# Paired softmax reciprocals, a common PSUM ring, QKV buffers for the first transform steps and a new task order

## The chip, the cores and the metric

The kernel runs on one core of one Trainium2 chip. Times are device microseconds of one execution. Runs come with a label: slow, when a run is over 1.5% above the fastest of the same kernel. On this kernel the times of one program spread evenly over some 2 to 3%, so that label cuts through one cloud; I give medians of all runs, and the ratios of fast runs beside them.

## The reference

Two independent halves share the output. Half A is a long convolution: a kernel K of 2048 taps for each of 1024 channels is built from complex exponentials, and u is convolved with it. Half B is attention in which each position sees 8 earlier ones at distance 2.

```python
P = jnp.exp(logdA[:, :, None] * l[None, None, :])
K = jnp.einsum("dn,dnl,dn->dl", Cc, P, dB).real
y = irfft(rfft(pad(K)) * rfft(pad(u)))[:L] + u * Dskip           # half A
q, k, v = split_heads(x @ wqkv)                                   # half B, 32 heads of 32
attn = softmax(where(mask, (q * k_gathered).sum(-1) * scale, -1e9))
out = concat([y, (attn @ v_gathered) @ wo], axis=-1)
```

## The kernel before

One program does both halves at once, as tasks put on the engines in a fixed order that is stored as a string (`ORDER`). The first part does the QKV projection (writing q, k, v to memory) beside the generation of K. A "shift" matmul group then finishes K, and a transform is done as matmuls: step 1 for u and for K (the tiles `z`), spectral products with constants `m` (`fwd`, product, `back`), and a last step. The attention (scores, exp, mask, values, reciprocal, product, output projection) is mixed into the spectral work.

```python
# first transform step, one group: 4 matmuls into a two-bank PSUM tile, then a copy
w["pz"] = cp().tile([128, 4, 256], F32, name="cp")
for i in range(4):
    nc.tensor.matmul(w["pz"][:, i, :], lhsT=src["t"][:, :, 4 * pi + i], rhs=self.l1[:, lk], ...)

# softmax denominators of one channel tile: exp(-ln(sum)), with a check sum
nc.scalar.activation(out=ln[:], in_=u["O"][:, 1, :], func=ACT.Ln, bias=self.tiny[:])
nc.scalar.activation(out=ln[:], in_=ln[:], func=ACT.Exp, scale=-1.0, accum_out=self.sums[:, 1, i:i + 1])
nc.vector.tensor_tensor(out=st["oT"][:, ct, :], in0=u["O"][:, 0, :], in1=ln[:], op=ALU.mult)

# constants of a spectral group: three buffers, loaded by GpSimd's queue
w["m2"] = self.mid.tile([128, 768], BF, name="m2", bufs=3)
nc.gpsimd.dma_start(out=w["m2"][:], in_=self.m2[p])
# [cut]
```

PSUM, eight banks: while QKV runs, three two-bank tiles (`ps`) for it and one (`cpl`) for the transform; afterwards two (`cp`) and one (`cpl`) in common and two single banks for attention's values.

Of the kernel before, what the change touches and what calls it, by code (L numbers as in the profile page):

```python
# [28 lines left out]
class Plan:  # L29
# [31 lines left out]
    "CQARAFwAgQE5AIkBIQAAAFAAlAGZAUEAGABpAWQAKQAdAmwASAAlAnEBMADsAPkBAQJID3wBoQFNAlEB0ADkABEC+AAMAlUCdQLwAAABDAEtAqEPqA8wAskB4QFgAn0CdAAYDrEBqAFZAbEPuA9AAngAiABkAYAA"  # L61
    "lADRATgCmADpAVEPWA/cAfQBSA7IDtwAEAFhD2gPcA+kAJ0CwA8cAagAuQEgAeEQoQ6lArQAxAEsAcAAvADoEPEQOAGoDlgCsQ4hDswA+Q4oDvgQNAF5DgAPgAIAEUQBMQ64DoAOqAKwAogCSAEZEMAOTAMJDzgO"
    "QA64AokOEA8YD5AOyQ8gENAPaAKQAsACyQLVAuAC3QLoAv0CJQMIAzAD8AIFA10DEAMtA0ADKRAwEHkPOAMYA4UDZQOQA2gDcAO1A5gOjQNVA1EOvQM4EMAD2Q/gD5gDgA/IA60DWA6JD6ADIQ+QD5gP/APoDywE"
    "2QM5EWEO5AMoD2gOcA4JBOwDMQ80BAQE0ANBBDgPOAR4A0AR0Q5ADyUF8Q/4D9gOSRFQES0FHARVBTUFCBHwA8kFSQThDlgRuRDoDvAOQRAUBDgFXARdBQEQCBDAEEgFQAVgBX0FaAVUBIgFyRCREBAQcAWlBUgQ"
    "hQVYEq0F1QVMBlEQuAWYBZEEkAWwBeAFaQSYBHAEeARhEcAF/QWABN0FWBDwBSUGoASYECAECAboBQUGXQYYBi0GEAZoBqgEiRGFBjgGuATQEGUGsATYEIgEcAYwBo0GQAZoEWAQwQSQEVUGcRHpBCAWyARgBPAE"
    "eAbQBPgEtQa9BtgE/AaQBqEQeBGAEQAFEAWoEMAGmAbIBpkRrQagEagRBAcREdkG4ATYERgFLAfQBuwGNAcJBzgH5AYlCGkQGBGwEPAGcBB5EIAQoAZhEmgSFAchEdkSQQfhEYgQLQjgEhwHcRKxEegRSQcoEQgF"
    "MBFcBzgIVQhUB8kI6RJpB3gSgBJdCJEHfQhgCDUICRJICEwJcAeYB2gIpQiICPEReAdACKAHhQhwCNUI4B6YCLAI8BKQCPgRrQjACLgI4AgBE4AHqAf9CN0IsAeIB+gICBMlCfgSBQnBBzAJEAm4EbgH8AhVCV0J"
    "LQnpBwASyAcQEggJwRHIEdAR8AcYCTgJ0AcxEvgHQAllCXAJGRJgB4UJkAloCY0JtQkgEtgHmAkgBwAICAgQCL0JERP8CcgJKBIYE60JIBM4EtETwAnQCUESSBJQEhgIKBYECikT2BPZCckL4RPoEzATCQosCjQK"
    "ORNAE4kSoAkhFDgKeAnsCSUL5AmgExwKkBLwEy0LQQoUCvAJmRJREygUWBN5E0kKoBJIE1UL4Ac4CzULSAtAC1wKVAqoEmALYRM1FGAKkQp9C2gTXQtpCrESpQtwC2gLhQuwC3AKiAs4FJgKoAqQC9ULmAutC8AL"
    "OBa4C3gKuBKACuAL/QvdC+gLJQyYFHATBQwIDIgKgBONExgM8AtAFMESyBKoCrAKqRNMDBAMMAyQE5gTXQxxFC0MOAy4CukKhQyNDEAM0BKYDMEKaAyQDLAT8Aq1DGUM6B6hFCAKyAqoFL0MyAygDNAKMBbADHAM"  # L70
    "uRPZDFUMeBR4DAkNgRT8DPgK0AzAE9gK+RMEDeQM7AzwDBwN8BUZFkAWQQ3IExQNABRMDVQNiBRJFJAUAAsQC+AKsRRQFBgLCAu4FGENiQ2tDGgNCRSQDcAUyRSYDXANoA14DSwNgA00DagN0BRAFeENuQ3oDcAN"
    "EBRxFRgUyA3wDdAN+A1ZFBAO8B7YDQAOWA2wDQgOOA0gDegVUhZZFjEXCBZaF0wWYRaFFogWkBb9FgAXSRXZFGAXGhggGHgVDB8IF6oXYBRoFIEVUBXgFLQXyheIFc0W6BTQFhkVWRXUF/oXIBUAGOoXkBUpFTAV"
    "8RT0FwoYtRbYFhAYYBWZFTgVaBW6F8AX+BTaFxUXwRXgFzoXuBagFQEVQBcYF4oX+B4IFRAVkBfIFWoX5RboFqkVcBfAFnoXnRagFtEVsBUgF4AXbRZwFpoXoBfwFkoXUBdAGLgV2BXgFSoYOBj4FWwqqRiwGDQY"
    "ABZpGBoZdBggGTkZiRiQGOoYRBlJGFAY9BjZGNoe+hgAGXkY5BiEGKkZqBYpGTAZChkUGbkYwBiZGKQYWRpaGGAYyRhYKnEqeSqBKkgZ1BiqKlEZsRlZLLEqwRnIGYwquRnKK2EacRrRK7wqkSrUGZkreBbdGWoa"
    "eBpZGaErhBqZKsEqjRppGeEZcBnpGQEaySpiGXwZkRqlKpkaCSvcK/AZEh+FGRErrCshHwka4SsZH9Qq6SvZKuEqCRscK4oZsSv4GbkrGRokGhEa9CshK6AalRlgKtUfxCuoGigaNRpFH+wqaStxKxIbIRsoG7Ea"
    "GRswGz0bfCuYGTkrQStMKzoa8SpBGvkqBCspKzQroBlhG4EtQRu6Go0fiS1IGsEayRpRK9Aa2BpqG7kbTRt5G1AbWBvlGnEbgSthLIAb6hpQGlkrjBtpLPEs8RpkK5Ub+SxIH8Eb0RsQFmkcyhv4GgAb+CvgG5kb"
    "2B8RHNwbcRx0LO0boRt6HPEb4B+ULYEciSuMHJAcUB+ZLZQrkSwaHPkbKRyQH50cmSwwHKgbLR95LCEcPBxFHMEcgSyhHMoc2RyNLLAbpCwZHSksMB/gHKEt0hypHL0fMCwAHDksCBxJHFEcwB+sLZgfIR0xHewc"
    "9RywHDgdcR2yLfkcBC1ALLktuBwFHQktKR0RLUgsRB1YHMkdCB0iLSktxC15HaksgR0cLVItAB+JHZAdmB3IH00dyS3RHaUdUR1ZLWAc4R3oHTgfsSylH7ws2h3wHV0fASyqHdEtdR8ILFkdeR4QHbUdZC1pLcEs"
    "gh4RLJEeIR79HckseB/ULJgeKR45HjEeSB6KHtAeRB6oHxgsYB+kHvEfaSBwIBkgACE6ICQgUCxAIIkhGSEgIZQh6iCpIDQt8CCZIdwtoCG0IHEtCiE5LSkgMCAUIbkh2iDgIEEuxCFJLnwtUS7pIfAhrR5aIWQh"
    "mS+4HaEvYB3ZLNkhICy5IEEtwCB6IOQhaSGEIMAdSSBwIWovSSFxL5ogVCCsL4kgaB1QIUwt4C0BHqAg4SxcLpQgyiApMA0esR5VHtAguR5ZIAogEB4YHikhYCAwIWEuFCA5IWkuRCF6LskhqSF1LoEu7CzQIREi"  # L80
    "tCH6HwAgsS95IfkhfC8IIvgguS+EIVoeACLZLuEujC5pImUegS8ZInEixC8pIjAigSKMIkoowB4iIpEuOCLsLnkiCS/IHpkulCJQKBIuWCgRL4kvpC6ZJ2gfOS/BIkEvySIcL6gnoCdoHnAeRSLZIuAiGC6dIiEu"
    "SSJRIugfcSOUL1giYCLRIkwvIS/yMPEuqS4pL+wiYCihIiguMC40L7EuvC5RL3kjiSMZI/kw+S5oKK0i6i2BI5AjMTAELzkw9SLwLVkvnCPBLiEjOC75IvktAC4xI7AiBDG4IkQwISQ4Iyoj0ShkL6UjSTCwJ8ku"
    "BSMII0AjcSgQI9Qu3ShRMHko4CgJMU0jCC5iMGkwdDCpI5EwsSO4I8Aj6CjSL5kwITERMV0wUSMpMVkjeTApJDkkgTA0McgvpDDJI9EkHDHYL+EvRCQxJIAoTCTZJKkwgjGxKIww6STwJBEyuCeJMbAf0SO5KOgv"
    "4iT4JDkxVSThI2Aj2SPsI7EwwTD0I/ovlDHJMPAvQTG8MFEx1DBMMVkkmTF5JFkx/SPAKGEkoTEFJdkwGTJkMWgjITI5M0EzADABJKwx4TAJJAkzDTBoJEwzLDLsMGkxKSURM4IkkSQQJCAwnCRwJAklcTGIKIkk"
    "ESUQMDEyMiUcMxgkOTJBJaQkfDFFMiEoOSVIJS0oUTOBJXoyUCWBMiEzSTIYJYklUTKtJJIlsSSZJaglpCWwMVwy2TLIKIwyWTPhMvkzvSTZJSAlujEpMzAoOCgYMGQzXSU0M2kzkTKZMsAkcTPAMckxtSWkMmEl"
    "0DFhMuwyqTJpMuEmbSWxMuIl2DF8M/EycCX5MsEn8SX8JekluiUAJs0ndDLIJAE06SaBMwk0xSXIJfEmMSZ4JfkmACfiJwgnvDIEM9AnDSbpJzE00CXBMjk0FDQRJokz8Cf4Jx0myTKUM+IxwTSAH0Q01DIZNFE1"
    "FSfoMck0WTUhNIkmkSahJhknSTRkNagmYTQgJjknIScoJggyaTT1MfgxUTQtNNQ0mia0JiE12TShM+E0dDRcNOw08jRpNfk0eTRxNb0mKTU6JtgngTSoMwEomDNJJgkoBDVUJnw1ADLhNbUzuDOMNJIokTSZNEEm"
    "KCcwJ1gmQCgJNUEnETXwKDQ1qSmdKKQ0USdcJ8ImHDXJJqk06TXxNak2ZSawKTk1EChKJ2kmsTZkJ7E0vDQ5N0E3/DVxJm0ngDVBNcozATYZNiE20DPwM7w2CTbZNsAz2TNMNcE2yTZMN+E2LDZSN7I1FTbsNlk3"
    "yTf6KBApeTbQJtQ2gTZkNzE24DOMNngm6DO4KfE2CTdJNrg1OTbYJoAmETccN3En+TZENsE1UTYAKaAokTYEN9I3fSchN8g12TfxOIAniTXAKZk2qCj5OFw2wjjkN6Q2YTYpNwQ5NDfJOJA10DXUOOo3GCkIKdg1"
    "aTZ0NvE3kjidNQk5/TcROdk4mThhOBw5cTekOKk4IjlpOOE4GCigNag1sTjIKew4vDh4N3Q4gSkpOTQ5gTeIN40pAjh5ODk5kCkxOAk4FDiBODk4mCmMONEpQTlCKU0pGThMOUQ42SmZNyIpUClYKSE4SThQOVE4"  # L90
    "XDjgKegpKSksODAptDmgNzEqOCmQN6k3sDfANz0qgjlhKbg3QCqIOUgqaSlZOfEpcCl4KZE5+SmYOQAqEioZKiAqKCpgOYgnKBegOQgqujmQJ2g3qDlpOXA5eDnEOVAqoCk="
# [403 lines left out]
RU = 256  # L495
NB = 4
# [6 lines left out]
SO = CP, ("O",) + CP  # L503
# [144 lines left out]
class Attention:  # L648
# [9 lines left out]
    def open_pools(self, ctx):  # L658
        pool = lambda n, b, **kw: ctx.enter_context(self.tc.tile_pool(name=n, side="right", bufs=b, **kw))
        cst = pool("t_c", 1); self.ld = pool("t_ld", 2); self.wk = pool("t_wk", 2); self.otp = pool("t_oT", 2)  # L660
        self.pp = pool("t_ps", 2, space=PSUM)
        self.mk = cst.tile([128, 2 * W0 + 64], BF, name="mk"); self.wo = cst.tile([128, 8, 1024], BF, name="wosb")
        self.sums = cst.tile([128, 2, 64], F32, name="sums")

    def load(self, ru, st):
        nc = self.tc.nc; f = 1 if ru % 4 == 0 else 0
        qs = self.ld.tile([128, 8, RU], BF, name="qs"); ks = self.ld.tile([128, 8, RU + 32], BF, name="ks"); vs = self.ld.tile([128, NB + 1, 512], BF, name="vs")
        nc.sync.dma_start(out=qs[:], in_=self.QT[ru])
        nc.sync.dma_start(out=ks[:, :, 32 * f:], in_=self.KT_[ru][:, :, 32 * f:])
        for h in range(2):  # L670
            nc.sync.dma_start(out=vs[64 * h:64 * h + 64, 1:, :], in_=self.Vd[ru * RU:ru * RU + RU, h, :].rearrange("(b k) x -> k b x", k=64))
            if not f:
                nc.sync.dma_start(out=vs[64 * h:64 * h + 32, 0, :], in_=self.Vd[ru * RU - 32:ru * RU, h, :])
        st.update(qs=qs, ks=ks, vs=vs)
# [14 lines left out]
    def exp(self, u):  # L689
        u["pe"] = self.wk.tile([128, 2, W0], BF, name="pe", bufs=3)  # L690
        self.tc.nc.scalar.activation(out=u["pe"][:], in_=u["S"][:, :, 0:W0], func=ACT.Exp, scale=SCALE, accum_out=self.sums[:, 0, u["i"]:u["i"] + 1])  # L691
# [5 lines left out]
    def values(self, ru, ct, st, u, bank):  # L697
        nc = self.tc.nc; first = ru % 4 == 0; ones = self.mk[:, 2 * W0:2 * W0 + 64]; pm = u["pe"]
        O = u["O"] = bank(self.pp, "O").rearrange("p (two q) -> p two q", two=2)
# [15 lines left out]
    def recip(self, u):  # L715
        ln = u["ln"] = self.wk.tile([128, RU], F32, name="ln")
        self.tc.nc.scalar.activation(out=ln[:], in_=u["O"][:, 1, :], func=ACT.Ln, bias=self.tiny[:])  # L717
        self.tc.nc.scalar.activation(out=ln[:], in_=ln[:], func=ACT.Exp, scale=-1.0, accum_out=self.sums[:, 1, u["i"]:u["i"] + 1])  # L718

    def norm(self, ct, st, u):  # L720
# [481 lines left out]
```

## Time and profile before

| | before |
|---|---|
| time | 523.11 us median of 4 runs (518.59 to 523.39) |
| span of the profiled run, clock | 517.9 us, 0.95 |
| TensorE busy | 449.4 us (87%) |
| ScalarE, VectorE busy | 406.2 us (78%), 385.2 us (74%) |
| K shift, first spectral matmul | 221.2 us, 272.4 us |

Busy shares alone would say that TensorE sets everything. The table of stages in the prediction says more: in one stretch of 51 us TensorE is slow in clock (0.83), and VectorE and ScalarE are idle for 61% and 44% of it.

### The profile page before, as it was taken

To read this page: it belongs to the slowest core of one execution; us is meant where nothing else is said; L and a number is where in the kernel's file an instruction comes from. 1 tells how busy PE (TensorE), PEld (TensorE's weight loads), DVE (VectorE), ACT (ScalarE), POOL (GpSimd) and SP (SyncE) were. 2 spreads that over 40 slices of the span, in tenths; PEclk is the share of its full clock that TensorE was granted. 3 is DMA by queue.
4 is the path that set the end of the run, shared out by engine and by line. 5 is a ranking of instruction groups with operands and counts; after the bars stand their busy time and mean duration, and the time that the engine had idled before them with its cause. 6 is when DMAs were issued, how large, how long until landed. Compare 5 with 4: busy or idle time off the path is not lost.

```text
span 517.9 us, 16566 instructions
## 1 busy us (share of the span) xinstructions
PE 449.4 (87%) x7056; PEld 238.9 (46%) x7118; DVE 385.2 (74%) x682; ACT 406.2 (78%) x738; POOL 34.8 (7%) x56
## 2 busy tenths in 40 slices
PE   4769999789999799779698788889997998998994
PEld 4544444444544345445474333476443443444541
DVE  2899999979899989515089897699773896784540
ACT  4779999996999988244769987799875986787863
POOL 1740000000000000010001010001000100000000
PEclk9979999899999899879879999999998998998998
DMA  8841333633416388545785787875779494788743
GB/s 290 274 131 45 81 88 106 140 73 118 104 48 154 93 160 251 119 131 132 173 212 127 246 207 241 272 218 145 197 223 237 128 260 131 183 235 223 223 143 108
DMA packets 110209, 86.39 MB, mean 167 GB/s; under 512 B 44896, under 2 KB 98912, under 8 KB 108848
## 3 DMA queue, kind: packets, MB, share of 16 engines
q1 hardware_dynamic: 106016, 73.91, 53.1%
q0 software_dynamic: 3024, 9.25, 6.3%
q10 hardware_dynamic: 1088, 2.10, 1.2%
q8 instruction: 57, 0.93, 0.8%
q14 instruction: 24, 0.20, 0.1%
HBM read 51.28 MB, written 33.95 MB: 165 GB/s over the span
## 4 chain that ended last, share of the span: by engine, by line
PE 34%; issue 9%; DMA 5%; DVE 5%; ACT 3%; POOL 1%; POOLq 0%; ACTq 0%
PE cp L755 8%; DMA m<-c_m 5%; PE cp L893 4%; PE ps L587 4%; PE cp L942 3%; PE cp L925 3%; PE cp L984 3%; PE O L712 3%; DVE z L467 2%; PE cp L686 2%; PE O L704 2%; ACT z L465 1%; POOL m L915 1%; DVE f L467 1%; ACT vs L465 1%
## 5 line engine op out<-in xcount | busy, mean ns | idle before, releaser
L587 PE MATMUL ps<-xT,w 128*128 128x512 bf16 x490 | 121.9, 397 | 4.9 <-ACT sg L465 2.3
L587 PEld LDWEIGHTS <-w 128*128 128x128 bf16 x512 | 50.4, 101 | 61.2 <-issue 10.7
L755 PE MATMUL cp<-wosb,oT 128*128 128x512 bf16 x232 | 59.0, 386 | 2.3 <-issue 1.4
L617 PE MATMUL ps<-wv,xT 128*128 128x512 bf16 x246 | 58.0, 381 | 2.1 <-DVE xT L467 1.2
L465 ACT CAST sg<-ps 128x1024 bf16<-128x1024 f32 x46 | 46.0, 1005 | 11.2 <-issue 5.1
L465 ACT CAST z<-cp 128x1024 bf16<-128x1024 f32 x38 | 38.0, 1014 | 18.3 <-PE cp L893 17.9
L925 PE MATMUL cp<-z,m 64*64 64x512 bf16 x512 | 39.0, 393 | 14.4 <-DMA m<-c_m 11.8
L467 DVE CAST z<-cp 128x1024 bf16<-128x1024 f32 x26 | 31.5, 1223 | 26.4 <-PE cp L893 26.1
L467 DVE CAST f<-cp 128x1024 bf16<-128x1024 f32 x28 | 34.2, 1223 | 17.7 <-PE cp L925 17.5
L893 PE MATMUL cp<-l,big 128*128 128x256 bf16 x256 | 39.8, 298 | 8.6 <-ACT z L465 5.0
L691 ACT ACTIVATE pe<-cp 128x576 bf16<-128x576 f32 x64 | 41.4, 648 | 6.3 <-PE cp L686 5.6
L465 ACT CAST f<-cp 128x1024 bf16<-128x1024 f32 x36 | 36.0, 1009 | 12.2 <-PE cp L925 11.8
L915 POOL DMA_DIRECT2D m<-c_m x32 | 17.3, 540 | 395.8 <-ACT kraw L465 188.9
L934 DVE TENSOR_TENSOR pr<-f 128x1024 bf16<-128x1024 bf16 x64 | 41.0, 684 | 1.1 <-ACT f L465 0.7
L893 PEld LDWEIGHTS <-big 128*128 128x128 bf16 x256 | 33.9, 173 | 15.6 <-issue 11.4
L617 PEld LDWEIGHTS <-xT 128*128 128x128 bf16 x256 | 24.6, 99 | 30.0 <-DVE xT L467 1.3
L695 DVE TENSOR_TENSOR pe<-pe,mk 128x576 bf16<-128x576 bf16 x64 | 28.4, 452 | 11.6 <-ACT pe L691 11.4
L755 PEld LDWEIGHTS <-oT 128*128 128x128 bf16 x256 | 23.0, 99 | 28.8 <-issue 4.8
L717 ACT ACTIVATE ln<-O,tiny 128x256 f32<-128x256 f32 x62 | 29.6, 477 | 8.1 <-PE O L712 7.9
L942 PE MATMUL cp<-pr,m 64*128 64x512 bf16 x256 | 33.7, 383 | 0.7 <-ACT f L465 0.5
L723 DVE TENSOR_TENSOR oT<-O,ln 128x256 bf16<-128x256 f32 x62 | 25.8, 419 | 10.6 <-ACT ln L718 9.6
L276 DVE SCALAR_TENSOR_TENSOR PH<-p_xs,p_phs 128x256 int32<-128x256 f32 x84 | 30.1, 419 | 0.6 <-ACT TL L285 0.6
(114 smaller groups left out, 731.1 us busy)
## 6 DMA issues: line engine op xcount, KB each, us to landing
Zv<-vs SPq DMA_DIRECT2D x64, 128.0 KB, 3.7
big<-Zv SPq DMA_DIRECT2D x32, 256.0 KB, 4.7
m<-c_m POOLq DMA_DIRECT2D x32, 192.0 KB, 3.6
Vt<-sg SPq DMA_DIRECT2D x32, 128.0 KB, 2.3
KT<-sg SPq DMA_DIRECT2D x16, 256.0 KB, 2.9
QT<-sg SPq DMA_DIRECT2D x16, 256.0 KB, 2.5
ud<-in_A_u_dram SPq DMA_DIRECT2D x16, 256.0 KB, 5.6
big<-ud SPq DMA_DIRECT2D x2, 2048.0 KB, 9.2
```

The source lines that it names most:

```text
L276: V.scalar_tensor_tensor(out=PH[:, j, :], in0=xc, scalar=float(RS[k + j] + 128), in1=self.phs[h][:, cs], op0=ALU.mult, op1=ALU.add)
L465: nc.scalar.copy(out=out, in_=in_)
L467: nc.vector.tensor_copy(out=out, in_=in_)
L587: nc.tensor.matmul(st["ps"][:, h, :], lhsT=self.w[ct // 2, t][:, kt, ct % 2 * 128:ct % 2 * 128 + 128], rhs=self.xT[:, kt, t0:t0 + 512], st ...
L617: nc.tensor.matmul(st["ps"][:, b, :], lhsT=self.xT[:, kt, t0:t0 + 128], rhs=self.wv[:, kt, :], start=(kt == 0), stop=(kt == 7))
L691: self.tc.nc.scalar.activation(out=u["pe"][:], in_=u["S"][:, :, 0:W0], func=ACT.Exp, scale=SCALE, accum_out=self.sums[:, 0, u["i"]:u["i"] ...
L717: self.tc.nc.scalar.activation(out=ln[:], in_=u["O"][:, 1, :], func=ACT.Ln, bias=self.tiny[:])
L755: nc.tensor.matmul(w["po"][:, h, :], lhsT=st["oT"][:, ct, tt * 128:(tt + 1) * 128], rhs=self.wo[:, ct, h * 512:(h + 1) * 512], start=(ct = ...
L893: nc.tensor.matmul(w["pz"][:, i, :], lhsT=src["t"][:, :, 4 * pi + i], rhs=self.l1[:, lk], start=True, stop=True, skip_group_check=True)
L925: nc.tensor.matmul(f[64 * ab:64 * ab + 64, c2, :], lhsT=t[rs, ab, o:o + 64], rhs=z[rs, 4 * p + 2 * ab + zi, :], start=(zi == 0), stop=(zi ...
L934: V.tensor_tensor(out=w["pr"][:, x], in0=w["f"][:, :, :, 0:256], in1=w["f"][:, x:x + 1, :, 256:512].to_broadcast([128, 2, 2, 256]), op=ALU ...
L942: nc.tensor.matmul(v[:, ab, :], lhsT=t[rs, k, :], rhs=w["pr"][rs, x, y].rearrange("p c d -> p (c d)"), start=(i == 0), stop=(i == 3), tile ...
```

## The change

It has four parts. (1) The denominators of two channel tiles are inverted by one Ln and one Exp, and normalised by one product; both outputs share one two-bank tile of the common ring, which gets a third `cp` buffer in place of the two single banks. (2) The first u steps may use the PSUM buffers of QKV. (3) Keys and queries are loaded in one task, V in a later one. (4) The order string is new; in it seven half-tiles of QKV (eight matmuls each) stand before the shift instead of after it.

```diff
-        self.pp = pool("t_ps", 2, space=PSUM)
-        ln = u["ln"] = self.wk.tile([128, RU], F32, name="ln")
-        activation(out=ln[:], in_=u["O"][:, 1, :], func=ACT.Ln, bias=self.tiny[:])
-        activation(out=ln[:], in_=ln[:], func=ACT.Exp, scale=-1.0, accum_out=self.sums[:, 1, i:i + 1])
+        ln = w["ln"] = self.wk.tile([128, 2, RU], F32, name="ln", bufs=LN_BUFS)      # LN_BUFS = 1
+        activation(out=ln[:], in_=w["O"][:, :, 1, :], func=ACT.Ln, bias=self.tiny[:])
+        activation(out=ln[:], in_=ln[:], func=ACT.Exp, scale=-1.0, accum_out=self.sums[:, 64 + i:65 + i])
-        tensor_tensor(out=st["oT"][:, ct, :], in0=u["O"][:, 0, :], in1=u["ln"][:], op=ALU.mult)
+        tensor_tensor(out=st["oT"][:, ct:ct + 2, :], in0=w["O"][:, :, 0, :], in1=w["ln"][:], op=ALU.mult)
 # first step
-                    w["pz"] = cp().tile([128, 4, 256], F32, name="cp")
+                    pool, n = psum(); w["pz"] = pool.tile([128, 4, 256], F32, name=n)
-                m = P("PE", 0.48, mm, [zh, l1], take=CP, ...)
+                m = P("PE", 0.48, mm, [zh, l1], take=("cpl", "ps") if hf == 0 and lk == 0 else CP, ...)
 # loads
+    def load_v(self, ru, st):      # the V part of load(), issued as its own task
-            st["cp"] = ...tile_pool(name="cp", side="right", bufs=2, space=PSUM)
+            st["cp"] = ...tile_pool(name="cp", side="right", bufs=3, space=PSUM)
 # [cut: the task list that goes with it, and the ORDER string]
```

## The prediction

> **What bounds the kernel now.** I began with the busy row and then cut the span into stages at events that the timeline shows: the start (to 39 us), QKV projection beside the generation of the convolution kernel K (39 to 208 and 208 to 221, where the last K values are drained), the first transform step with leftover QKV matmuls between (221 to 272.4, where the first spectral matmul starts), then spectral work, attention and output projection mixed until 507, and the tail. This is the stage table of the kernel before; columns are stretch, length, busy us of PE, PEld, DVE, ACT, POOL with instruction counts, granted clock, DMA share, GB/s.
>
> ```profile
> 0.00:39.00 39.00, 23.71 (x193) 18.26 (x196) 27.82 (x42) 25.11 (x33) 17.55 (x24) 0.91 0.71 231
> 39.00:208.00 169.00, 158.55 (x2284) 78.25 (x2307) 158.59 (x304) 158.21 (x258) 0.00 (x0) 0.97 0.46 113
> 208.00:221.00 13.00, 9.59 (x404) 5.71 (x405) 6.48 (x11) 2.98 (x6) 0.00 (x0) 0.87 0.50 102
> 221.00:272.40 51.40, 42.71 (x271) 28.62 (x274) 19.90 (x39) 28.60 (x32) 1.63 (x3) 0.83 0.67 165
> 272.40:340.00 67.60, 56.55 (x1048) 27.60 (x1049) 56.48 (x105) 57.16 (x107) 7.01 (x13) 1.00 0.75 219
> 340.00:403.00 63.00, 56.32 (x982) 31.38 (x976) 46.76 (x66) 50.89 (x101) 4.31 (x8) 0.97 0.75 205
> 403.00:507.00 104.00, 98.07 (x1895) 47.48 (x1916) 68.98 (x118) 80.29 (x204) 4.31 (x8) 0.97 0.68 188
> 507.00:518.00 11.00, 3.85 (x19) 1.61 (x18) 0.14 (x1) 2.94 (x3) 0.00 (x0) 0.81 0.30 103
> ```
>
> TensorE is busy 449.4 of 517.9 us, so only its 68.8 us of idle time and its slow clock can be won: 15.3 us idle in the start, 10.5 to 208, 3.4 to 221, 8.7 to 272.4, 11.1 to 340, 6.7 to 403, 5.9 to 507, 7.2 in the tail. From 39 to 208 all three engines are at 94%: nothing is free there. The stretch 221 to 272.4 is the odd one: VectorE works 19.9 of 51.4 us, ScalarE 28.6, and TensorE's clock is only 0.83. The waits of all engines and the timeline say why:
>
> ```profile
> ACT z L465 <- PE cp L893: 17.9, 20, 3.3
> DVE z L467 <- PE cp L893: 26.1, 9, 13.9
> ```
>
> The two evacuating engines sit 44 us waiting for first-step matmuls, 41.7 of them in this stretch. In the chain of waits, between 225 and 252 us, a group of four such matmuls (0.44 us) alternates with eight QKV matmuls (1.73 us): at that point the first step has one two-bank PSUM buffer, because the others open only once QKV has closed its own. From 272 on, TensorE's waits are short and mostly for the constants m:
>
> ```profile
> PE cp L925 <- DMA m<-c_m: 11.8, 12, 3.0
> ```
>
> **What the Trainium skill says.** "ScalarE: Activation LUTs", section "What ACT_TABLE_LOAD costs", gives an ACTIVATE as a fixed part plus 0.833 ns an element: a merged instruction keeps one fixed part. The trace agrees in slope: the copy of 1024 takes 1005 to 1014 ns and the Ln of 256 takes 477, 0.69 ns an element apart over different functions; I use 0.83. "VectorE: DVE Perf Modes", section "Why PSUM operands drop a tier", says fp32 from PSUM runs at the single rate; the 1024-element copy at 1223 ns and the 256-element product at 419 differ by 1.05 ns an element, which agrees. "PSUM — Partial Sum Buffer", "Specifications (TRN2)", gives eight 2 KiB banks; before, 2x2 (cp) + 2 (cpl) + 2x1 (O) use them all, after, 3x2 + 2 do. "TensorE: Matmul & The Clock Gate", "What's actually happening", says the clock is halved after an idle window; the trace shows 28 first-step matmuls taking 5.94 us (212 ns each) at 259 us, against 0.44 us for four (110 ns) earlier.
>
> **The change, part by part.** These are the rows concerned, from the groups by shape:
>
> ```profile
> L717 ACT ACTIVATE ln<-O,tiny 128x256 f32<-128x256 f32 x62 | 29.6, 477 | 8.1 <-PE O L712 7.9
> L718 ACT ACTIVATE ln<-ln 128x256 f32<-128x256 f32 x64 | 26.7, 417 | 2.0
> L718 ACT ACTIVATION_READ_ACCUMULATOR ln<-ln 128x1 f32 x64 | 11.9, 186 | 0.0
> L723 DVE TENSOR_TENSOR oT<-O,ln 128x256 bf16<-128x256 f32 x62 | 25.8, 419 | 10.6 <-ACT ln L718 9.6
> ```
>
> *Pairs.* One tile costs ScalarE 477 + 417 + 186 = 1080 ns, 64 tiles 69.1 us. A pair should cost (477 + 256x0.83 = 690) + (417 + 213 = 630) + 186 = 1506 ns, 32 pairs 48.2 us: 20.9 us less ScalarE work, about 5 us in 272 to 340, 16 us after. The VectorE product goes from 64x419 = 26.8 to 32x(419 + 256x1.05 = 688) = 22.0 us, 4.8 us less. TensorE's instructions are the same in number and shape. As TensorE is the bound, this is no 21 us of span; it buys shorter waits in the 23.7 us of idle time between 272.4 and 507. PSUM: the one-bank outputs go, two tiles share a two-bank buffer of a common ring with one buffer more. A pair holds it from its first value matmul through about 1.5 us of reciprocal and 0.7 us of product, some 4 us with the second tile's matmuls; 32x4 = 128 us over four buffers in 235 us leaves the rest the equivalent of 3.5 buffers instead of 3. This is a mild gain, with the danger that a held pair blocks the ring.
>
> *First u steps.* They may also take the QKV buffers (three more), and the order moves QKV ahead. Counted in TensorE's program order: after the K shift, 11 half-tiles of eight QKV matmuls stand between first-step groups before, 4 after; 7 half-tiles, 7x1.73 = 12.1 us, move to before 221 us. The stretch after the shift then holds 4x1.73 + 128x0.11 + about 2 for the shift = 23 us of TensorE work at full clock instead of 35. Evacuation for it (32 z tiles, about 18 on ScalarE and 14 on VectorE, 4 of QKV, the K placements of about 6 us on VectorE) is 22 us of ScalarE and 23 of VectorE. With start and fill latencies I take 32 us instead of 51.4: 19.4 won. The 12.1 us must be paid before 221, where TensorE idled 13.9 us since 39. Much of that idle time is the wait for K's producers or too early to fill; I let 4 us go into it, so the shift comes 8 us later. Net 11 us.
>
> *Keys and queries apart from V.* Scores can start on a load of two tensors while V follows. No large wait of TensorE on these loads is listed before, so I give it nothing by itself; it makes the other order possible.
>
> *New order in the spectral part.* The load of m has three buffers, so group p+3's load starts when group p's inverse matmuls are done. I added up TensorE work lying between these points, using the matmul spacings of the trace (0.07 us forward, 0.12 inverse, 0.216 projection): before, 15 of 29 loads have under 5 us of cover, after, 14, the missing sum falls from 23.0 to 18.5 us, and the last 16 have 7.7 us of cover on average instead of 6.5. Landing takes 2.6 to 8.3 us, so I take 2 us of the 11.8 away. From slack on ScalarE, the fourth buffer and a little more clock I take another 4 us. Net 6 us here.
>
> Sum: 11 + 6 = 17 from about 521 us (the runs before lie at 518.6 to 523.4), so 504. The new order is dense and I know none of its waits; I give back 2 us for waits that I can't name and predict 506.
>
> **Rivals.** (1) *The work moved ahead isn't absorbed.* From 39 to 208 TensorE, ScalarE and VectorE are all at 94%, and the QKV drains move with the matmuls (about 3.5 us of ScalarE). If none of the 12 us fits, and the last K values come later still through ScalarE, the first part gains 5 us or less: 511 to 514. For it: the 94%. Against it: the 13.9 us idle, and that 208 to 221 was slow through clock 0.87, not through ScalarE at 3 of 13 us. (2) *The pair becomes the wait.* Two tiles must be ready for one Ln, the ln tile now has one buffer, and a held two-bank output stalls scores and forward matmuls behind it. If each of 32 pairs costs TensorE 0.4 us, 13 us go: 517 to 519, about the time of before. For it: in the new order the two value groups of a pair are up to 3.2 us of TensorE work apart. Against: most lie within 0.4 to 1.6 us, and successive pairs start 5 us apart on average. (3) *DMA holds the second half.* The DMA share is 0.68 to 0.75 there and the bytes don't change; if waits for m and for the round trip of Zv through memory stay as they are, all of the 6 us fail: 510 to 512. (4) *All idle time but the start and tail shrinks by half*, as smoother feeding also lifts the clock from 0.83: 498.
>
> **Range and chances.** 2% under 521 is about 511. The central path and rival 4 lie below it, rival 3 on it, rivals 1 and 2 above. None of them gets above 523 unless two meet. I take 497 to 516 as the range for 8 in 10, 0.66 for faster, 0.31 for the same, 0.03 for slower.
>
> **What would show it.** Right: Ln near 690 ns and the second Exp near 630, 32 of each; the stretch from the K shift to the first spectral matmul at 30 to 35 us with the waits of ScalarE and VectorE on first-step matmuls well under 25 us together; the shift at 225 to 231 us; TensorE's idle time between first spectral matmul and 11 us before the end at 16 to 19 us, TensorE's total busy time within 1% or lower. Wrong: the shift later than 233 us (rival 1); TensorE waiting over 8 us on the Ln, the normalising product or a buffer they hold (rival 2); waits for m at 12 us or more (rival 3).

## The result

The changed kernel takes 507.06 us (median of 4 runs, 502.91 to 512.25) against 523.11. The ratio of the fast runs is 0.9686 (95% interval 0.9597 to 0.9775). A ratio here is the mean time of one kernel's fast runs over that of the other's in the same rounds, so it isn't quite the ratio of the medians.

The stage table of the changed kernel has the same columns as that of before. Its shift comes at 224.7 us and its first spectral matmul at 252.9 us, so the cuts lie there; the next two stretches are as long as before.

```profile
0.00:39.00 39.00, 21.53 (x184) 16.47 (x185) 26.09 (x41) 22.14 (x28) 16.39 (x21) 0.95 0.65 211
39.00:208.00 169.00, 166.60 (x2261) 80.83 (x2259) 163.92 (x306) 161.39 (x263) 1.90 (x4) 0.99 0.52 126
208.00:224.70 16.70, 13.72 (x520) 8.06 (x519) 6.78 (x10) 4.50 (x7) 1.08 (x2) 1.00 0.46 93
224.70:252.90 28.20, 24.54 (x239) 19.61 (x238) 20.61 (x42) 22.67 (x26) 0.55 (x2) 1.00 0.82 216
252.90:320.50 67.60, 55.35 (x1034) 25.23 (x1034) 50.45 (x94) 51.82 (x90) 7.09 (x13) 0.90 0.78 234
320.50:383.50 63.00, 56.41 (x925) 33.59 (x926) 45.50 (x57) 45.69 (x74) 3.77 (x7) 0.92 0.59 167
383.50:490.20 106.70, 104.50 (x1948) 49.88 (x1947) 73.03 (x105) 76.74 (x152) 4.85 (x9) 1.00 0.71 204
490.20:501.20 11.00, 3.85 (x20) 1.56 (x18) 0.14 (x1) 2.94 (x3) 0.00 (x0) 0.91 0.30 103
```

The stretch between shift and first spectral matmul has shrunk from 51.4 to 28.2 us, with the clock back at 1.00, though 12 us of QKV matmuls are now done before the shift, which itself comes only 3.5 us later: TensorE's idle time from 39 us to the shift fell from 13.9 to 5.4 us. From the first spectral matmul to the end it is the other way round: 245.5 us before, 248.3 us after. TensorE's idle time there fell a little (from 23.7 to 21.0 us without the tail), but the granted clock fell from 1.00 and 0.97 to 0.90 and 0.92 in the first two stretches. So 19.5 us came from the first part, and the second gave 2.8 us back. The first figure repeats: the control below has its first spectral matmul at 253.7 us. The second is within the scatter: the second half of the same program took 254.0 us there.

The waits of the changed kernel, over the whole span (engine, line and tile, releaser: us in total, times, longest), that answer to those of before:

```profile
PE cp L935 <- DMA m<-c_m: 10.8, 6, 3.6
ACT z L464 <- PE cp L902: 3.3, 3, 1.5
DVE z L466 <- PE cp L902: 1.0, 4, 0.3
```

The 44 us of waits for first-step matmuls are down to 4.3. Those for m are as long in total as before, but there are 6 instead of 12. The longer ones cost a second time, in the matmuls that follow. This is from the timeline of TensorE in the changed kernel (start, us, engine, line, operation, tile, shapes, count, idle time before and its releaser):

```profile
277.94 1.92 PE L935 MATMUL cp<-z,m 64*64 64x512 bf16 x16 [2.25 <-DMA m<-c_m]
...
289.26 1.06 PE L935 MATMUL cp<-z,m 64*64 64x512 bf16 x16
```

Sixteen matmuls of the same shape take 1.92 us after a wait of 2.25 us and 1.06 us when TensorE has been fed for a while.

The groups by shape for the pairs (same columns as before):

```profile
L721 ACT ACTIVATE ln<-cp,tiny 128x512 f32<-128x512 f32 x32 | 22.1, 692 | 10.7 <-PE cp L716 9.7 <-DVE oT L727 0.8
...
L727 DVE TENSOR_TENSOR oT<-cp,ln 128x512 bf16<-128x512 f32 x32 | 22.0, 688 | 19.8 <-ACT ln L722 17.5 <-PE cp L764 2.0
...
L722 ACT ACTIVATE ln<-ln 128x512 f32<-128x512 f32 x32 | 20.1, 630 | 1.0
...
L722 ACT ACTIVATION_READ_ACCUMULATOR ln<-ln 128x1 f32 x32 | 6.0, 186 | 0.0
```

A pair costs 692 + 630 + 186 = 1508 ns of ScalarE and 688 ns of VectorE, as worked out beforehand. ScalarE's total fell from 406.2 to 387.9 us, some 14 us of it after the first spectral matmul. None of it is seen in the second half's time.

### The profile page after: what moved, and what is told of

Same layout as the page of the kernel before. It is cut to its first block, busy times and chain, and to the rows that moved or that the text cites.

```text
span 501.2 us, 16502 instructions
## 1 busy us (share of the span) xinstructions
PE 446.5 (89%) x7118; PEld 235.2 (47%) x7118; DVE 386.5 (77%) x652; ACT 387.9 (77%) x640; POOL 35.6 (7%) x56
## 4 chain that ended last, share of the span: by engine, by line
PE 49%; issue 26%; ACT 9%; DMA 9%; DVE 3%; POOL 1%; SPq 1%; POOLq 0%; ACTq 0%; DVEq 0%
PE ps L586 14%; PE ps L616 9%; PE cp L764 7%; PE cp L952 4%; PE cp L935 3%; DMA m<-c_m 3%; PE pk L376 3%; PE cp L994 3%; PE cp L716 2%; ACT ER L303 2%; DMA xn<-in_B_x_dram 2%; ACT OR L284 2%; PE cp L708 2%; ACT sg L464 2%; PE cp L688 2%
## 5 line engine op out<-in xcount | busy, mean ns | idle before, releaser
L586 PE MATMUL ps<-xT,w 128*128 128x512 bf16 x512 | 118.3, 380 | 0.8 <-ACT sg L464 0.6
L764 PE MATMUL cp<-wosb,oT 128*128 128x512 bf16 x256 | 61.9, 386 | 0.0
L935 PE MATMUL cp<-z,m 64*64 64x512 bf16 x512 | 40.5, 423 | 12.9 <-DMA m<-c_m 10.8
L925 POOL DMA_DIRECT2D m<-c_m x32 | 17.3, 542 | 380.9 <-ACT kraw L464 182.7
L466 DVE CAST f<-cp 128x1024 bf16<-128x1024 f32 x26 | 31.7, 1222 | 12.1 <-PE cp L935 11.8
L727 DVE TENSOR_TENSOR oT<-cp,ln 128x512 bf16<-128x512 f32 x32 | 22.0, 688 | 19.8 <-ACT ln L722 17.5
L952 PE MATMUL cp<-pr,m 64*128 64x512 bf16 x256 | 36.3, 409 | 0.5 <-ACT f L464 0.3
L902 PEld LDWEIGHTS <-big 128*128 128x128 bf16 x256 | 30.1, 174 | 6.5 <-issue 4.8
L548 PE MATMUL ps<-idn,xn 128*128 128x128 bf16 x176 | 16.9, 277 | 17.5 <-ACT sg L464 6.9
L464 ACT CAST z<-cp 128x1024 bf16<-128x1024 f32 x29 | 27.9, 1032 | 3.6 <-PE cp L902 3.3
L721 ACT ACTIVATE ln<-cp,tiny 128x512 f32<-128x512 f32 x32 | 22.1, 692 | 10.7 <-PE cp L716 9.7
L902 PE MATMUL cp<-l,big 128*128 128x256 bf16 x212 | 27.8, 275 | 2.4 <-ACT z L464 1.7
```

The lines of the kernel that those rows point to most:

```text
L464: nc.scalar.copy(out=out, in_=in_)
L466: nc.vector.tensor_copy(out=out, in_=in_)
L586: nc.tensor.matmul(st["ps"][:, h, :], lhsT=self.w[ct // 2, t][:, kt, ct % 2 * 128:ct % 2 * 128 + 128], rhs=self.xT[:, kt, t0:t0 + 512], st ...
L764: nc.tensor.matmul(w["po"][:, h, :], lhsT=st["oT"][:, ct, tt * 128:(tt + 1) * 128], rhs=self.wo[:, ct, h * 512:(h + 1) * 512], start=(ct = ...
L935: nc.tensor.matmul(f[64 * ab:64 * ab + 64, c2, :], lhsT=t[rs, ab, o:o + 64], rhs=z[rs, 4 * p + 2 * ab + zi, :], start=(zi == 0), stop=(zi ...
L952: nc.tensor.matmul(v[:, ab, :], lhsT=t[rs, k, :], rhs=w["pr"][rs, x, y].rearrange("p c d -> p (c d)"), start=(i == 0), stop=(i == 3), tile ...
```

## The experiments

Four questions. Is the pairs' saving off the path? Do the waits for m explain the missing gain of the second half? Which of the two edits to the first part makes its gain? What do the V load and the ring do? Twelve kernels were run in three sets; all outputs were correct. Each set ran on another chip, with the kernel before beside it: medians 520.81, 519.46 and 517.84 us. The argument rests on profiles and on medians that lie far apart.

### The yardstick, pairs taken apart, a fourth buffer for m

**Control.** The changed kernel again.

> The changed kernel again, unchanged, as the yardstick of the other runs on this chip. All theories: ratio to before 0.965 to 0.975 (about 505 to 508 us).

It took 502.93 us (493.79 to 509.58, six runs), ratio 0.9616, from the two runs that count as fast. That is just below the range expected; the medians give 0.966, within it. The effect repeats. The profiled run, 509.58 us, had 18.5 us of waits for m instead of the 10.8 of the run above: most of the first-part numbers repeat (shift at 225.2, first spectral matmul at 253.7 us), and the second half varies.

**Pairs taken apart.**

```diff
+        for c in range(2):
-            activation(out=ln[:], in_=w["O"][:, :, 1, :], func=ACT.Ln, ...)
+            activation(out=ln[:, c], in_=w["O"][:, c, 1, :], func=ACT.Ln, ...)
 # the Exp and the product likewise, one check sum for each
```

> The changed kernel with the reciprocal and the normalising product of a pair done as two instructions of 256 each again, in the same places of the same order (same PSUM, same tasks). ScalarE gets back 20.9 us and VectorE 4.8 us of work. Theory A (both engines are off the path in the second half; TensorE and its waits for m set it): within 2 us of the control, ratio to before 0.966 to 0.974. Theory B (the merged instructions are what the change lives on): 8 us or more slower than the control, ratio 0.985 or more.

It took 501.17 us (median of six), 1.8 us less than the control and within its scatter; ratio 0.9666. Between the first spectral matmul and the tail, ScalarE was busy 186.7 us in its profile, against 174.4 in the control's: 12.3 us more rather than 20.9, as neighbouring instructions overlap in part and the sum of their durations counts that twice (in the timeline at 301 to 303 us, each read of the check sum starts 0.1 us before its Exp ends, and the next Ln 0.1 us before the read ends). The time didn't notice. Theory B is out. The run keeps both outputs in one PSUM tile, so it tests the merged instructions and not the pairing in PSUM.

**A fourth buffer for m, in the changed kernel and in the one before.**

```diff
-                    w["m2"] = self.mid.tile([128, 768], BF, name="m2", bufs=3)
+                    w["m2"] = self.mid.tile([128, 768], BF, name="m2", bufs=4)
-                w["S"] = self.kt.tile([128, 8, 128], BF, name="S", bufs=2)
+                w["S"] = self.kt.tile([128, 8, 128], BF, name="S", bufs=1)      # makes the room
```

> The changed kernel with four buffers instead of three for the constants m (room made by one buffer less for S, which is used twice, far apart). Theory A (in the second half six waits of 0.2 to 3.6 us for m, 10.8 us in all, and the half-clock matmuls after them, ate the expected gain): 8 to 14 us faster than the control, waits of TensorE for m under 3 us, granted clock between the first spectral matmul and 130 us later back at 0.97 or more. Theory C (pairs held in PSUM or lack of work make those waits; another wait takes their place): less than 3 us faster.

> The kernel before with the same fourth buffer for m. Theory A: its 11.8 us of waits for m go too, but they were short (3.0 us at most) and the clock stayed at 1.00, so 5 to 10 us faster than before, ratio 0.980 to 0.990, and the changed kernel with four buffers beats it by 18 us or more. Theory C: ratio 0.995 or more.

The changed kernel took 493.78 us (491.67 to 498.08), 9.2 us less than the control; the kernel before took 509.63 us, 11.2 us less than without the buffer (5 to 10 were expected). The buffer taken from S goes with it in both and was not tested apart. The waits of TensorE for m, changed kernel:

```profile
PE cp L935 <- DMA m<-c_m: 0.9, 1, 0.9
```

and before, where one is left:

```profile
PE cp L925 <- DMA m<-c_m: 4.4, 1, 4.4
```

So the fourth buffer is worth some 10 us in both kernels, though in the one before a wait of 4.4 us stays. That was the part of theory A that fell: I had expected them to explain why the second half of the changed kernel shows no gain, with a lead of 18 us or more once they were gone. The lead is 15.8 us (17.9 without the buffer). The stage tables with four buffers, first spectral matmul to 11 us before the end, show it. The changed kernel:

```profile
253.40:321.00 67.60, 56.61 (x1094) 28.77 (x1098) 53.74 (x98) 54.95 (x96) 7.09 (x13) 0.96 0.85 240
321.00:384.00 63.00, 59.71 (x1052) 35.65 (x1057) 50.36 (x66) 51.80 (x87) 4.31 (x8) 0.98 0.71 192
384.00:480.90 96.90, 92.38 (x1738) 44.28 (x1752) 64.49 (x93) 66.94 (x134) 3.77 (x7) 1.00 0.69 199
```

and the kernel before:

```profile
272.70:340.30 67.60, 58.10 (x1028) 28.92 (x1029) 55.83 (x105) 55.99 (x106) 6.99 (x13) 0.95 0.77 222
340.30:403.30 63.00, 58.57 (x1033) 32.77 (x1036) 50.46 (x73) 54.11 (x111) 4.30 (x8) 1.00 0.73 195
403.30:498.30 95.00, 91.59 (x1841) 45.47 (x1860) 65.62 (x113) 77.28 (x194) 3.76 (x7) 1.00 0.74 205
```

TensorE is busy 208.7 of 227.5 us in the one and 208.3 of 225.6 in the other. ScalarE has 13.7 us less to do in the changed kernel (173.7 against 187.4), and TensorE's idle time isn't smaller (18.8 against 17.3 us). It is now made of many waits under 1 us and a few on other transfers. The clock did return: 0.96 and 0.98, where the control's profile has 0.92 and 0.92.

How exact this is, another run of the same program shows, the yardstick of the third set:

```profile
252.30:319.90 67.60, 59.86 (x1111) 30.50 (x1115) 55.51 (x100) 57.16 (x98) 7.09 (x13) 0.95 0.83 248
319.90:382.90 63.00, 59.33 (x1104) 34.57 (x1110) 50.66 (x67) 50.44 (x89) 4.32 (x8) 1.00 0.68 185
382.90:475.60 92.70, 89.64 (x1672) 42.87 (x1683) 62.42 (x89) 66.03 (x131) 3.77 (x7) 1.00 0.72 208
```

Here TensorE idles 14.5 us, and from the first spectral matmul to the end it is 234.3 us, against 238.5 us in the run above and 236.6 us in the kernel before with four buffers. The kernel before lies between two runs of one program: the second half shows no gain and no loss beyond this scatter of about 4 us.

### The two edits to the first part, one at a time and both

For these I re-encoded the order string: engine queues as in the changed kernel, except for the tasks named, and tasks emitted in the first order that the buffers allow.

```diff
 # e2_one_buffer
-                m = P("PE", 0.48, mm, ..., take=("cpl", "ps") if hf == 0 and lk == 0 else CP)   # rings as chosen in ORDER
+                # every u step takes "cpl"
 # e2_qkv_back: TensorE's queue after the shift
-  s1, ..., QKV half, s1 x5, QKV half, s1, QKV half, s1 ...    (4 halves after the shift)
+  s1, QKV half, s1, QKV half, ...                             (11 halves after the shift, as before)
 # e2_first_part_back: both
```

> The changed kernel with its first u steps in the one two-bank buffer that they had before, all orders on the engines kept. Theory A (the first part gains because 12 us of QKV matmuls moved into idle time AND the u steps no longer alternate on one buffer): sixteen groups now cycle at 0.44 us of matmuls + 1.0 to 1.2 of copy + about 0.2, some 28 us instead of 15.3 for the u steps, less what the four QKV halves between hide; the stretch from shift to first spectral matmul grows from 28 to 36 to 40 us, 8 to 11 us slower than the control (ratio 0.980 to 0.985). Rival D (moving QKV is all): under 3 us slower.

> The changed kernel with the 7 half-tiles of QKV put back after the K shift, between the u steps as before; the u steps keep the QKV buffers. Theory A: the idle time before the shift comes back in part (PE idle 39 us to shift from 5 to 10 or more), the shift comes at 217 to 221 us instead of 225, the stretch after it takes 38 to 42 us; 6 to 9 us slower than the control (ratio 0.976 to 0.982). Rival E (the buffers are all; work is only moved from one side of the shift to the other): shift at 213, total within 2 us of the control.

> Both of these together: one buffer for the u steps and the 7 half-tiles after the shift, so the first part is that of before in a kernel that keeps the pairs, the common ring with one buffer more, the separate V loads and the new order of the second half. Theory A (the whole gain is in the first part): first spectral matmul at 266 to 273 us, ratio to before 0.99 to 1.005. Rival F (the second half gained too): 0.985 or less.

The medians were 525.68, 519.03 and 533.07 us (five runs each), so 23, 16 and 30 us above the control of the first set (this set had none of its own). Of the five runs of the first only one, 514.15 us, counts as fast, and no ratio was given; its profiled run, 522.45 us, is labelled slow. The ratios of the other two are 1.0131 and 1.0323. The stretches from the shift to the first spectral matmul, control:

```profile
225.20:253.70 28.50, 24.72 (x234) 19.53 (x233) 20.53 (x42) 22.67 (x26) 0.59 (x2) 1.00 0.81 223
```

one buffer:

```profile
225.40:274.30 48.90, 32.08 (x234) 22.99 (x234) 21.09 (x42) 23.45 (x26) 0.60 (x2) 0.76 0.52 148
```

QKV back:

```profile
221.70:266.00 44.30, 36.89 (x287) 25.46 (x290) 21.19 (x42) 26.54 (x30) 1.63 (x3) 1.00 0.59 152
```

both:

```profile
222.20:282.50 60.30, 43.17 (x291) 28.20 (x297) 21.32 (x42) 27.03 (x30) 1.62 (x3) 0.86 0.48 134
```

*QKV back* does what theory A says, by somewhat more. The shift comes at 221.7 us instead of 225.2, not 12 us earlier: TensorE's idle time from 39 us to the shift rises from 7.9 to 14.6 us, and the stretch afterwards grows by 15.8 us, to 44.3 where 38 to 42 were expected. Rival E is out. The total loss was larger than the 6 to 9 us expected, 12.3 us of it by the first spectral matmul.

*One buffer* loses twice what I had expected. The timeline of TensorE shows why:

```profile
254.45 1.01 PE L901 MATMUL cp<-l,big 128*128 128x256 bf16 x4 [1.10 <-ACT z L463]
256.78 1.01 PE L901 MATMUL cp<-l,big 128*128 128x256 bf16 x4 [1.31 <-DVE z L465]
258.89 1.01 PE L901 MATMUL cp<-l,big 128*128 128x256 bf16 x4 [1.10 <-ACT z L463]
```

With one buffer and no QKV matmul between, TensorE waits for every copy; and with waits of 1.1 to 1.3 us between groups of four, those groups take 1.01 us instead of 0.60, so the cycle is over 2 us instead of 1.7. The clock of the stretch is 0.76 (0.50 from 250 to 265 us), though no wait of a matmul in it was longer than 1.6 us. In the kernel before, eight QKV matmuls stood between the groups until 252 us and covered most of these copies. Moved away, they leave the u steps of one buffer with nothing to cover them; with the extra buffers that does no harm.

*Both* missed its expectation (0.99 to 1.005 for theory A): at 1.0323 it is slower than before. The first spectral matmul came at 282.5 us, 10 us later than in the kernel before, because my order within this stretch (60.3 us against 51.2) isn't the searched one of before: 12.5 us of waits on copies of ScalarE are listed in it. But the rest agrees better with theory A than with rival F. From the first spectral matmul on, this kernel, with pairs, ring, split loads and the new order, takes 250.1 us, against 245.5 in the kernel before. A gain in the second half isn't there. The order of the second half was never put back by itself, so its share isn't known.

*What each edit is worth.* As my order alone costs something, the fair base is *both*, not the kernel before. From its 533.07 us, keeping the extra buffers gains 14.0 us (*QKV back*), keeping the moved QKV 7.4 us (*one buffer*), and keeping both, in the changed kernel, 30.1 us. The first spectral matmul comes at 282.5 us, then at 266.0, 274.3 and 253.7. So each edit helps, and the two together by more than their sum; as the changed kernel also has the searched order, the excess over the sum isn't shown to be theirs. Against the kernel before (272.4 us), extra buffers alone bring the first spectral matmul 6.4 us forward, and QKV moved alone 1.9 us back.

### A try at the start

```diff
 # e2_start_m4, on top of the four buffers: ScalarE's queue at 30 us
-  sine of TL (waits for VectorE), copy of V
+  copy of V, sine of TL
```

> A try at a faster version: four buffers for m, and one copy of V on ScalarE put ahead of a sine that waits 4.8 us for VectorE, so that the transposes at 32 us don't wait 6.2 us for its PSUM. If TensorE sets the first part, up to 4 us faster than with m alone (ratio 0.942 to 0.950 to before); if VectorE and ScalarE set it, as their 92 per cent from 39 us on allow, less than 1.5 us.

It took 493.62 us, ratio 0.9587, like the fourth buffer alone (493.78 us in the set before). The shift came at 226.0 us, as without it. The wait of 6.2 us was gone, to 0.9 us, but the next matmuls of V then waited 7.0 us, instead of 0.4, for VectorE's copy of x, which stands behind other work in its queue: one wait took the place of the other. Whether TensorE or the other two engines set the first part is left open by this run.

### On the quieter base: pairs, V load, ring

These four all have the fourth buffer for m, which shrinks the scatter of a kernel to some 1.3%.

```diff
 # e3_m4_joint_load
         st.update(qs=qs, ks=ks)
+        self.load_v(ru, st)                       # and the task of V does nothing
 # e3_m4_ring
-            st["cp"] = ...tile_pool(name="cp", side="right", bufs=3, space=PSUM)
+            st["cp"] = ...tile_pool(name="cp", side="right", bufs=2, space=PSUM)
 # e3_m4_split: as e1_split
```

> The changed kernel with four buffers for m again, the quieter yardstick for this set: 492 to 496 us, ratio to before 0.945 to 0.960.

> The same with the pair's instructions taken apart again (20.9 us of ScalarE and 4.8 us of VectorE work more). Theory A (off the path): within 2.5 us of the yardstick also where no wait for m hides it. Theory B: 8 us slower or more.

> The same with V loaded in the place where keys and queries are, as before. Theory A (each matmul waits only for its own tile, so the split moves only the place in the queue): within 2.5 us of the yardstick. Rival G (V loads in front of the queue wait for their buffer and hold stores and later loads back): 4 us slower or more, with waits of TensorE on loads of ks, big or m that the yardstick lacks.

> The same with one buffer less in the common PSUM ring of the second half (two and one instead of three and one, orders on the engines kept). Theory A' (the fourth buffer only makes up for what the pairs occupy, 0.5 of a buffer on average, and the old split of three plus two single banks was as good): 8 to 20 us slower, all of it after the first k step. Theory H (PSUM is not scarce in the second half at all): less than 4 us slower.

| kernel | median us (six runs) | ratio to before, 95% interval |
|---|---|---|
| yardstick | 490.33 | 0.9498 (0.945 to 0.9545) |
| pairs apart | 492.68 | 0.9510 (0.9465 to 0.9555) |
| V with k and q | 498.15 | 0.9628 (0.9586 to 0.9669) |
| one ring buffer less | 568.63 | 1.1014 (1.0967 to 1.1062) |

The yardstick came out 1.7 us below its expected range, with the ratio inside its own. It is the fastest kernel of this study; it beats both kernels of the case by changing two buffer counts.

*Pairs apart* costs 2.3 us, with intervals that overlap, for 12.4 us of busy time on ScalarE (186.0 against 173.6 us in the second half). Theory A holds.

*V with k and q* costs 7.8 us. Some of that lies before the shift (227.5 us against 223.9), where the two programs are the same, so it is scatter (the other profiles with QKV moved lie between these two); the six runs of each don't overlap, though. From the first spectral matmul on it is 239.9 against 234.3 us, which is 5.6 us. The waits in its profile, and the one that caused them:

```profile
DVE vs L466 <- DMA Zv<-vs: 5.8, 2, 3.1
PE cp L936 <- DVE vs L466: 5.1, 2, 3.2
```

The yardstick has 1.7 and 0.9 us in these two, and in SP's queue its four loads of V at 272.1 us come behind the stores of spectral results that start at 265.6 us; here the four loads come first (269.9 us), and the stores start at 272.5 us (the whole half runs 3.8 us later here, so some 3 us of this is delay). Four V loads in the queue ahead of the stores of spectral results hold those stores back, the staging tile `vs` isn't free, its copy is late, and TensorE waits for the PSUM buffer behind it. Rival G is supported, though its waits turn up on a store instead of on ks, big or m.

*One ring buffer less* costs 78 us, far beyond the 8 to 20 expected. TensorE's waits are then on whoever holds the ring, first of all for the output projection:

```profile
PE cp L763 <- ACT pe L692: 8.0, 6, 2.2
PE cp L763 <- DVE oT L726: 6.0, 3, 2.3
```

In this order the second half can't give up a PSUM buffer. That the pairs eat what the additional buffer brings may be a reason why this part gained nothing, but it isn't shown: a version with pairs, or without, in the PSUM layout of the other needs its own searched order, and an order made for four buffers suffers more with three than one made for them would.

## Why the prediction was right

Point by point, by its own steps.

- **Pairs.** The sizes of one instruction were right to 1% (692, 630, 186 and 688 ns); their sum, 20.9 us of ScalarE, was too large, because it counted overlaps: 12.3 us of busy time. The prediction's reading that 0.69 ns an element "agrees" with 0.83 was none, as it compared two functions; the result gives 0.84 for Ln and 0.83 for Exp. That they would buy no 21 us of span was right too; taken apart, they cost 0 to 2.3 us. The step that let them still help, through "slack on ScalarE, the fourth buffer and a little more clock", 4 us, did not show: TensorE's idle time in the second half, with four buffers for m, is 18.8 and 14.5 us in two runs of the changed kernel and 17.3 us in the kernel before.
- **First u steps and QKV moved.** The mechanism was right, and both halves of it are needed for the whole gain, as the experiments showed. The size was too small: 11 us predicted, 19.5 measured. Two terms were mis-sized. I let 4 of 12.1 us go into idle time; the idle time before the shift fell by 8.5 us, and the shift came 3.5 us later instead of 8. And I took 32 us for the stretch; it took 28.2. It fell below the 30 to 35 us that I had named as the sign.
- **Keys and queries apart from V.** "I give it nothing by itself" was wrong: put back, it costs about 5.6 us, through stores held back in the queue. As there was no such wait in the profile of before, whose order was made for the joint load, the split seems a part of making the new order work, as the prediction also said, rather than a gain over the old one.
- **New order in the spectral part.** Here the step failed. I took 2 of 11.8 us of waits for m away; in the profiled run 10.8 us are left, in the control's 18.5. Adding up the cover in front of each load pointed the right way for their number, 6 instead of 12, and said nothing of their length. The longer waits also slowed the clock, to 0.90 and 0.92, which I hadn't counted. The predicted 6 us of gain became a loss of 2.8 us in the profiled pair. This is rival 3, where the transfers hold the second half: its sign, 12 us or more of waits for m, was just missed in the profiled run and met in the control. TensorE's idle time there, 21.0 us, also missed the 16 to 19 named as the sign of being right. But it isn't the whole cause: with four buffers for m, and nearly no such waits, the second half shows no gain either, and why stays open.
- **The sum** (17 us, less 2 for unnamed waits; measured 16.7 us between the profiled spans and 16.1 between the medians) is right because the first part gave 8.5 us more and the second 8.8 us less than said. That these two errors cancel is luck. Rival 1 (the moved work isn't absorbed) and rival 2 (pairs become the wait; only 0.8 us of ScalarE's waits are for the one ln tile, and 1.7 us of TensorE's for the normalising product) didn't come about. Rival 4 didn't either.

## What to carry to other kernels

Work that covers another step's copies is also its buffer: before moving it away, give that step more PSUM. Shortening an engine that isn't the bound bought nothing measurable here; look instead at which buffer or transfer the bound engine's longest waits name, and price a wait of 1 to 2 us on TensorE at more than its length, since the matmuls after it can run at half rate. When loads share a queue with stores that free staging tiles, their place in the queue matters, though no matmul waits for the loads.

## What the Trainium skill lacked or had wrong

- "TensorE: Matmul & The Clock Gate", section "What's actually happening", gives an idle window of about 3.4 us as what slows the clock. Here waits of 1.1 to 1.6 us, repeated, took the clock of a 48.9 us stretch to 0.76 (0.50 for 15 us of it), and waits of 1.78 and 2.25 us, 6 us apart, were followed by matmuls at 120 ns instead of 66 (1.92 and 1.06 us for 16). The section "A second HAM failure mode: psum-queue depth-cycling" does name short idling between matmul groups, and the run with one buffer agrees with it; it gives no length of wait. These runs do, though no single length decides: of four waits of 2.06 us in the run with both edits undone, two were followed by QKV matmuls at full rate (1.89 us for eight) and two by slower ones (3.19 us for eight, 1.37 us for four).
- "ScalarE: Activation LUTs" gives the cost of an ACTIVATE but none for the read of its accumulator: 186 ns after each Exp of the reciprocals, whether it summed 256 or 512 elements, and 199 to 203 ns after each Exp of the scores. Its 0.833 ns an element is confirmed: with 256 elements more, Ln grew from 477 to 692 ns (0.84 each) and Exp from 417 to 630 ns (0.83 each).
- "PSUM — Partial Sum Buffer" calls its 2 MiB tight without a price: one two-bank buffer less of four cost 78 us of 490 in this kernel, in an order made for four.
